# Routed attention and a gated conv FFN on one core: heads prepared in pairs, argmax out of PSUM, shared banks, weights cast on engines, and a new order

## The chip, the cores and the metric

The kernel runs on one core of one Trainium2 chip. The metric is the device time of one launch in microseconds; the kernel before takes 281.45 us (median of three runs, 280.99 to 282.95). Engines are named as in the profile: PE (TensorE, matmuls), PEld (its weight loads), DVE (VectorE), ACT (ScalarE), POOL (GpSimd) and SP (SyncE, which here only issues DMAs). Only PE writes PSUM with matmuls; DVE and ACT read it.

## The reference

Four batches of eight heads, 768 tokens, head size 64; 16 centroids for each head. Queries and keys attend only within their own cluster; the attention output feeds an FFN with a three-tap convolution as its gate. Everything is given in float32.

```python
q_assign = np.argmax(np.einsum('bhsd,hcd->bhsc', q_n, c_n), axis=-1)
k_assign = np.argmax(np.einsum('bhsd,hcd->bhsc', k_n, c_n), axis=-1)
mask = q_assign[:, :, :, None] == k_assign[:, :, None, :]
scores = np.where(mask, scale * np.matmul(q, k.transpose(0, 1, 3, 2)), -1e9)
attn = softmax(scores)                    # over the keys
x = np.matmul(attn, v)                    # -> (4, 768, 512)
h = np.maximum(x @ w_in, 0.0)             # 512 -> 1024
conv_out = sum(conv_w[k] * shifted(h, k - 1) for k in range(3))
return (h * sigmoid(conv_out)) @ w_out    # 1024 -> 512
```

## The kernel before

**Preparing a head.** Each of the 32 heads is loaded by SP into one tile, q and k side by side (`load_q`, `load_k`, L272 and L275: the tile takes pieces of 64 floats, 256 bytes), and v into another (L279). PE transposes six 128x128 blocks against the identity into PSUM (`transposes`, L287). Two copies bring them to SBUF as `qkT` (`qkT_copy`: 512 columns on DVE, L296; 256 on ACT, L294). GpSimd casts to float16 into `ext`, the operand of the scores, directly for the first eight heads (L301) and otherwise into `c16` (L304), from where SP shifts the halves into `ext` by DMA (L306). PE multiplies with the normalised centroids (`assign`, L315, four matmuls that the profile lists as eight).

**The argmax.** DVE transposes the similarities within PSUM (L328), takes the maximum over 16 centroids (L337), compares (L341), multiplies with a descending index (L345), takes the maximum again (L347), and writes codes of the cluster to a small tile `pack` (L349, L351, L355). PE turns `pack` (L360), DVE copies the result (`spk`, L365), and a DMA writes it as three more rows of `ext` (L366). Those rows add to a score a number that is near zero where the clusters agree and very negative elsewhere, so that the exp needs no mask.

**Attention.** The work is cut into 32 slots, one for each batch, query half and head pair. A slot has six steps of scores (two matmuls of 384 columns into one of two double banks `sc`, L424), each followed by an exp on ACT (L436), and six value groups of six matmuls (L442) into the bank `avb`, one slot later. DVE normalises (L454, L455), PE transposes back (L465) and DVE copies into `xT` (L469). The slots go through the four head pairs with one query half and then again with the other, so that heads 0 to 7 serve slots 0 to 7.

**FFN.** When the pairs of a query half are done, eight tiles of the first layer follow (`ffn_in`, L484, into the bank `fp`), each with a relu (L499 on ACT, L497 on DVE), three taps on DVE (L518, L520; at the end on PE, L536), a tanh on ACT (L550), a gate on DVE (L554); the output layer is L560, with a copy out (L572 on ACT, L574 on DVE) and a store by SP (L575). The weights come from DRAM by DMAs that GpSimd issues and that cast on the way (L657, L662).

**PSUM.** Four banks have owners: `tra` and `trb` for preparation, `avb` for values, `fp` for the FFN.

**Order.** Nothing is scheduled automatically: `SLOTS` lists for each slot the steps of all engines in program order, and each engine executes its own in that order. A step waits for the data it needs; what stands behind it on that engine or queue waits too.

Of the kernel before, what the change touches and what calls it, by code (L numbers as in the profile page):

```python
# [801 lines left out]
```

## Time and profile before

| | us |
|---|---|
| median of three runs | 281.45 |
| the profiled execution, span | 281.0 |
| PE busy | 256.6 |
| DVE busy | 233.8 |
| ACT busy | 211.1 |
| POOL busy | 85.7 |
| 16 DMA engines, share of the span, queue of SP | 41.3% |

The slices show a span in 40 parts of 7 us, with the busy share in tenths. The groups list instructions of one line, with the mean duration of one and the idle time ahead of them. The chain follows the last instruction back, at each step to what released it. The timeline lists instructions in order of time, and windows give the busy time of all engines in a stretch. A group's mean includes some 0.1 us in which the next instruction of the engine has already begun, so sums of means lie above the busy time.

### The profile page before, as it was taken

The page shows a single profiled execution, that of the slowest core. Times are in us where ns is not written, and L with a number is a line of the kernel's source. Part 1 is how long each engine was busy: PE and PEld are TensorE (multiplying, and loading weights), DVE is VectorE, ACT ScalarE, POOL GpSimd, SP SyncE. Part 2 cuts the span into 40 slices and gives each one's busy share as a digit, 9 for nine tenths or more (in the row PEclk, how much of TensorE's full clock was granted, in tenths as well). Part 3 has the DMA queues.
Part 4 walks back from the last instruction along what each step waited for, and adds up shares of the span by engine and source line. Part 5 has one row for each costly group of instructions (what it writes and reads, how often), then busy time and mean ns, then how long its engine had stood idle before and what let it go on. Part 6 is the DMA issues. An engine that isn't in the chain of part 4 may idle for free.

```text
span 281.0 us, 7068 instructions
## 1 busy us (share of the span) xinstructions
PE 256.6 (91%) x2605; PEld 160.4 (57%) x2605; DVE 233.8 (83%) x648; ACT 211.1 (75%) x337; POOL 85.7 (30%) x183
## 2 busy tenths in 40 slices
PE   4887695899998999999999989999999999999991
PEld 1444353566755667766666656566566576565540
DVE  4578785478999999999999989989999898897441
ACT  2344584368998979989898879979899999973421
POOL 5783568012326224033563160052142000200000
PEclk9999999579999999999999999999999999999998
DMA  8965549934639468237625765248242110112104
GB/s 162 269 127 90 152 92 166 220 86 110 162 74 158 127 150 219 51 86 182 170 76 137 195 160 126 58 120 220 66 136 56 41 40 0 40 38 77 59 16 149
DMA packets 65816, 32.78 MB, mean 117 GB/s; under 512 B 53491, under 2 KB 62707, under 8 KB 65782
## 3 DMA queue, kind: packets, MB, share of 16 engines
q1 hardware_dynamic: 62184, 29.46, 41.3%
q0 software_dynamic: 2304, 2.10, 5.6%
q10 hardware_dynamic: 1294, 0.77, 0.9%
q8 instruction: 20, 0.33, 0.5%
q14 instruction: 14, 0.11, 0.1%
HBM read 23.11 MB, written 6.29 MB: 105 GB/s over the span
## 4 chain that ended last, share of the span: by engine, by line
PE 69%; DVE 20%; DMA 4%; ACT 3%; issue 2%; DVEq 0%; ACTq 0%
PE sc L424 18%; PE fp L560 10%; PE fp L484 10%; PE avb L442 9%; DVE cnv L520 5%; PE trb L315 4%; PE tra L287 3%; PE sc L560 3%; PE trb L287 3%; DMA ext<-spk 3%; DVE qkT L296 2%; DMA qk_in<-in_k_dram 2%; PE sc L536 2%; PE tra L465 2%; DVE val L345 2%
## 5 line engine op out<-in xcount | busy, mean ns | idle before, releaser
L436 ACT ACTIVATE attn<-sc 128x768 f16<-128x768 f32 x192 | 148.8, 820 | 12.7 <-PE sc L424 11.5
L424 PE MATMUL sc<-ext 128*128 128x384 f16 x384 | 92.3, 335 | 5.0 <-DMA ext<-spk 3.9
L520 DVE SCALAR_TENSOR_TENSOR cnv<-hpad,cwcol,cnv 128x382 f16<-128x382 f16 (+1 forms) x108 | 64.7, 617 | 0.2
L442 PEld LDWEIGHTS <-attn 128*128 128x128 f16 x1152 | 52.7, 99 | 13.8 <-issue 1.9
L442 PE MATMUL avb<-v,attn 128*128 128x65 f16 x1152 | 57.6, 195 | 0.1
L424 PEld LDWEIGHTS <-ext 128*128 128x128 f16 x384 | 33.2, 99 | 26.6 <-issue 11.4
L484 PE MATMUL fp<-xT,w_in 128*128 128x384 f16 x220 | 45.0, 325 | 0.8 <-ACT hpad L499 0.8
L560 PE MATMUL fp<-w_out,hg 128*128 128x512 f16 x144 | 39.2, 379 | 0.0
L554 DVE SCALAR_TENSOR_TENSOR hg<-th,hpad 128x764 f16<-128x764 f32 (+2 forms) x33 | 30.2, 925 | 6.9 <-ACT th L550 6.9
L304 POOL CAST c<-qkT 128x768 f16<-128x768 f32 x24 | 21.7, 906 | 43.0 <-issue 16.9
L309 POOL CAST v<-v_in 128x384 f16<-128x384 f32 x32 | 15.9, 510 | 56.0 <-DMA v_in<-in_v_dram 35.9
L484 PEld LDWEIGHTS <-w_in 128*128 128x128 f16 x256 | 22.8, 97 | 15.6 <-issue 3.3
L499 ACT ACTIVATE hpad<-fp 128x384 f16<-128x384 f32 x51 | 25.7, 504 | 6.1 <-PE fp L484 5.6
L294 ACT ACTIVATE qkT<-trb 128x256 f32<-128x256 f32 x30 | 11.6, 386 | 23.2 <-PE trb L287 8.8
L296 DVE COPY qkT<-tra 128x512 f32<-128x512 f32 x30 | 20.5, 682 | 7.0 <-PE tra L287 6.8
L560 PEld LDWEIGHTS <-hg 128*128 128x128 f16 x192 | 17.1, 97 | 15.5 <-issue 1.2
L550 ACT ACTIVATE th<-cnv 128x764 f32<-128x764 f16 (+1 forms) x27 | 23.1, 855 | 0.1
L287 PE MATMUL tra<-id,qk_in 128*128 128x128 f32 x120 | 20.2, 295 | 1.1 <-DMA qk_in<-in_k_dram 1.1
L455 DVE TENSOR_TENSOR x<-avb,rec 128x384 f16<-128x384 f32 x32 | 17.8, 558 | 1.1
L315 PE MATMUL trb<-qkT,cT 128*32 128x192 f32 x240 | 17.0, 357 | 1.9 <-ACT qkT L294 1.1
L287 PEld LDWEIGHTS tra<-id,qk_in 128*128 128x128 f32 x120 | 15.4, 152 | 5.3 <-issue 2.3
L518 DVE TENSOR_SCALAR cnv<-hpad,cwcol 128x382 f16<-128x382 f16 (+1 forms) x54 | 17.6, 340 | 0.0
(107 smaller groups left out, 287.1 us busy)
## 6 DMA issues: line engine op xcount, KB each, us to landing
qk_in<-in_q_dram SPq DMA_DIRECT2D x32, 192.0 KB
v_in<-in_v_dram SPq DMA_DIRECT2D x32, 192.0 KB
qk_in<-in_k_dram SPq DMA_DIRECT2D x31, 192.0 KB
out_dram<-o_sb SPq DMA_DIRECT2D x22, 256.0 KB
ext<-c SPq DMA_DIRECT2D x48, 96.0 KB
w_in<-in_moe_w_in_dram POOLq DMA_DIRECT2D x8, 128.0 KB, 4.5
w_out<-in_moe_w_out_dram POOLq DMA_DIRECT2D x8, 128.0 KB, 6.9
out_dram<-o_sb ACTq DMA_DIRECT2D x2, 256.0 KB
```

Of the source, the lines that this page charges most:

```text
L287: nc.tensor.transpose(to, qk_t[h][:, j].rearrange("p a d -> p (a d)"), id128[:])
L296: nc.vector.tensor_copy(out=to, in_=bank)
L315: nc.tensor.matmul(sims[32 * j : 32 * (j + 1), :], lhsT=cT32[:, h % H, :], rhs=tokens[:, j], start=True, stop=True, skip_group_check=True,)
L424: nc.tensor.matmul(s[:, i, 0:HS], lhsT=ext_b[h % NE][:, 1, P * (kt + i) : P * (kt + i + 1)], rhs=ext_b[h % NE][:, 0, HS * a : HS * (a + 1) ...
L436: nc.scalar.activation(attn[t, g // 3][:, kt : kt + 2, :], bank_of.pop((t, g))[:, :, 0:HS], AF.Exp, scale=0.125)
L442: nc.tensor.matmul(avp[:, u, 0 : D + 1], lhsT=attn[t, hd][:, kt, P * jq : P * (jq + 1)], rhs=v16_b[(h0 + hd) % NE][:, kt, 0 : D + 1], star ...
L484: nc.tensor.matmul(bank[:, 0:HS], lhsT=w_in16[:, r, 2 * u + f, :], rhs=xT[:, b % 2, r, HS * a : HS * (a + 1)], start=(r == 0), stop=(r == ...
L499: nc.scalar.activation(to, bank[:, 0:HS], AF.Relu)
L520: nc.vector.scalar_tensor_tensor(out=cnv, in0=src, scalar=w, in1=cnv, op0=ALU.mult, op1=ALU.add)
L550: nc.scalar.activation(th_t[n][:, fs, 0:N], pre[:, fs, 0:N], AF.Tanh, scale=0.5)
L554: nc.vector.scalar_tensor_tensor(out=o[:, fs], in0=th_t[n][:, fs, 0:N], scalar=1.0, in1=h[:, fs], op0=ALU.add, op1=ALU.mult)
L560: nc.tensor.matmul(bank[:, 0:Dm], lhsT=hg_b[b][:, fb, P * tq : P * (tq + 1)], rhs=w_out16[:, fb, :], start=(fb == 0), stop=(fb == NFB - 1) ...
```

## The change

The kernel is written anew around head pairs. `PLAN` replaces `SLOTS`: one list of steps, in which `T.3.1@0` is the second group of four transposes of pair 3 into bank 0, `S`/`E`/`V` scores, exps and values, `I`/`O`/`U` the two FFN layers, `Qa`/`Qd`, `Ra`/`Rd`, `Ya`/`Yd`, `Fa`/`Fd` copies, relus and so on with their engine (ACT or DVE), and `_wl`, `_wp`, `_wd`, `_wa` a weight's load and its cast on GpSimd, DVE or ACT.

- **Loads.** One DMA brings q, k or v of two heads (pairs 0 and 1: q and k of one head each). Runs are 768 bytes for q (three tokens) and 1536 for k and v, on both sides. A transposed block now holds two tokens, so the casts and shifts into `ext` write runs of 128 elements (256 bytes) for even and odd blocks; four heads are cast directly (GpSimd, ACT, DVE), 28 by `c16` and DMA. Queries now lie in another order, which the copy into `xT` undoes by writing with a stride of three.
- **Chunks.** A pair's 1536 columns of `qkT` are three copies of 512: 32 on ACT and 16 on DVE in all.
- **Argmax.** The transpose writes to SBUF, all steps but that one read SBUF, the comparison and the product are float16, and each step covers two heads (384 elements; the first four heads one by one). One scaling step is gone (a factor in `scalar2`); a turn and its copy serve two heads.
- **Banks.** `tra`, `trb`, `avb` and `fp` become `flex0` to `flex3`, and `PLAN` names the bank of each use.
- **Weights.** SP loads float32 blocks into buffers that later hold other tiles; 16 casts follow on GpSimd (9), DVE (4) and ACT (3).
- **Engines.** 28 relus are on DVE (9 before) and 36 on ACT; the copies into `xT` are 16 and 16 (all on DVE before); the output copies 12 and 12 (6 and 18 before). The six warm-up matmuls on zeros are gone.

```diff
-SLOTS = {
-    0: (
-        "S0 E0 @zd/10 M1/2 D/3 M2/2 LV/4 S1 M0/3 LK/5 M3/2 LQ/5 M1/3 @wi/1 LQ/6 Ta/4 E1 M4/2 Tb/4 @v/9 QA/4 M5/2 M2/3 "
...
+PLAN = (
+    "E.0.0 K.1.1@2 T.3.1@0 M0.2 CQ.2.1 S.0.1 _wa.2 B.1.1 T.4.0@3 M1.2 BA.1.1 _wp.3 S.0.2 Qd.3.1 E.0.1 CX.2.0 "
...
-    tra = psum.tile([P, 512], F32, name="tra")
-    trb = psum.tile([P, 512], F32, name="trb")
-    avb = psum.tile([P, 512], F32, name="avb")
-    fp = psum.tile([P, 512], F32, name="fp")
+    flex = [psum.tile([P, 512], F32, name=f"flex{i}") for i in range(4)]
+    bank = [x[:] for x in flex] + [sc[i // 2][:, i % 2, :] for i in range(4)]
...
-    def load_q(hh):
-        nc.sync.dma_start(qk_in(hh)[:, :, 0], q[hh // H, hh % H].rearrange("(j p) d -> p j d", p=P))
+    def load_q(g, h=None, queue=nc.sync):
+        b, h0 = batch_pair(g)
+        hs = heads(h)
+        queue.dma_start(
+            qk_in(g)[:, 0, hs].rearrange("p h (a j) d -> p (h a) (j d)", a=2),
+            q[b, h0 + hs.start : h0 + hs.stop].rearrange("h (a p j) d -> p (h a) (j d)", a=2, p=P),
+        )
...
+    def transposes(g, c, at):
+        chunk_at[g, c] = at
+        for i in range(4):
+            h, j = divmod(4 * c + i, J)
+            blocks = qk_t[g][:, j // 3, h, 2 * (j % 3) : 2 * (j % 3) + 2].rearrange("p j d -> p (j d)")
+            nc.tensor.transpose(bank[at][:, P * i : P * (i + 1)], blocks, id128[:])
...
-        for a in range(2):
-            nc.sync.dma_start(ext_b[h % NE][0:D, a, :], c[a * D : (a + 1) * D, :])
+    def ext_blocks(g, h, i):
+        return ext_b[g % NE][0:D, h].rearrange("p a (j t s) -> p t (a j) s", t=2, s=P)[:, i]
...
+    def shift_qk(g, h):
+        c = c_t.pop((g, h))
+        for i in range(2):
+            nc.sync.dma_start(ext_blocks(g, h, i), c[i * D : (i + 1) * D, :].rearrange("p (n s) -> p n s", s=P))
...
-    def sims(h):
-        tb = where[h][1]
-        nc.vector.transpose(tb[:, 0:192], tb[:, 256:448])
...
+        if i == 0:
+            sim_t[key] = rot.tile([P, 384], F32, name="sim", tag="sim", bufs=1)
+            nc.vector.transpose(sim_t[key][:, 0 : G * C], bank[sims_at[key]][:, 0 : G * C])
+        elif i == 1:
+            mx_t[key] = rot.tile([P, 24], F32, name="mx", tag="mx")
+            sim = sim_t[key][:, 0 : G * C].rearrange("p (u c) -> p u c", c=C)
+            nc.vector.tensor_reduce(out=mx_t[key][:, 0:G], in_=sim, axis=AX.X, op=ALU.max)
+        elif i == 2:
+            eq_t[key] = rot.tile([P, 24, C], F16, name="eqq", tag="eqq", bufs=1)
...
+            nc.vector.tensor_tensor(out=eq_t[key][:, 0:G], in0=sim, in1=mx, op=ALU.is_equal)
+        elif i == 3:
+            val_t[key] = rot.tile([P, 24, C], F16, name="val", tag="val", bufs=1)
...
+            nc.vector.tensor_tensor(out=val_t[key][:, 0:G], in0=eq_t.pop(key)[:, 0:G], in1=iota, op=ALU.mult)
...
+    def xT_copy(t, on_act):
+        b, a, pr, g = slot(t)
+        to = xT[:, b % 2, pr, HS * a : HS * (a + 1)].rearrange("p (s j) -> p j s", j=3)
+        src = bank16[x_at[t]][:, 0:HS].rearrange("p (j s) -> p j s", j=3)
...
-            nc.gpsimd.dma_start(
-                w_in16[:, r, f].rearrange("p fb f -> p (fb f)"),
-                moe_w_in[r * P : (r + 1) * P, f.start * P : f.stop * P],
-            )
+    def load_weights(i):
+        if i < 4:
+            nc.sync.dma_start(w_t[i], moe_w_in[P * i : P * (i + 1), :])
+            return
...
+        if name == "wa":
+            nc.scalar.activation(to, src, AF.Copy)
+        else:
+            (nc.gpsimd if name == "wp" else nc.vector).tensor_copy(out=to, in_=src)
```

Three places of the order follow; rows name line, operation, output and inputs, with the size.

SP, the DMA queue, from the shifts of pair 2 to the bias rows of pair 3, in the change (`c` to `ext` is a shift of one head, `spk` to `ext` are bias rows, `w_sb` is a block of weights):

```order
L311 DMA ext_90<-c_345 64x6x128 x2
L311 DMA ext_90<-c_382 64x6x128 x2
L587 DMA w_sb<-in_moe_w_in_dram 128x1024
L271 DMA v_in<-in_v_dram 128x2x384
L255 DMA qk_in<-in_q_dram 128x4x192
L263 DMA qk_in<-in_k_dram 128x2x384
L382 DMA ext_90<-spk 3x12x128 x2
L311 DMA ext_91<-c_488 64x6x128 x2
L311 DMA ext_91<-c_506 64x6x128 x2
L382 DMA ext_91<-spk 3x12x128 x2
```

The same place before, around the bias rows of heads 6 to 8:

```order
L366 DMA ext_91<-spk 3x12x128
L275 DMA qk_in<-in_k_dram 128x6x64
L272 DMA qk_in<-in_q_dram 128x6x64 x2
L275 DMA qk_in<-in_k_dram 128x6x64
L366 DMA ext_92<-spk 3x12x128
L275 DMA qk_in<-in_k_dram 128x6x64
L272 DMA qk_in<-in_q_dram 128x6x64 x2
L279 DMA v_in<-in_v_dram 128x384 x2
L366 DMA ext_93<-spk 3x12x128
```

The bias rows went by head between loads of one head; they now go by pair behind a weight block and the loads of a pair, and the weights stand in SP's queue instead of GpSimd's.

ACT around its first exps, in the change (`qkT` is a chunk copy, `w_in` a weight cast, `attn` an exp):

```order
L293 ACTIVATE v_2_96<-v_in 128x12x64
L382 DMA ext_88<-spk 3x12x128
L287 ACTIVATE qkT<-flex_71 128x512
L608 ACTIVATE w_in_78<-w_sb 128x512
L287 ACTIVATE qkT<-flex_69 128x512
L287 ACTIVATE qkT<-flex_68 128x512
L382 DMA ext_89<-spk 3x12x128
L411 ACTIVATE attn<-sc_66 128x768
L608 ACTIVATE w_in_78<-w_sb 128x512
L382 DMA ext_89<-spk 3x12x128
L411 ACTIVATE attn<-sc_67 128x768
```

Before, the first two exps stood behind two bias-row DMAs and six copies, and no cast; now two casts of loaded v, two casts of weights and four bias-row DMAs stand ahead of or between them.

DVE, from the last argmax of a single head to that of pair 2, in the change:

```order
L365 SCALAR_TENSOR_TENSOR pack_101<-best,pack_101 128x2x6
L289 COPY qkT<-flex_71 128x512
L340 STREAM_TRANSPOSE sim<-flex_69 128x384
L377 COPY spk<-flex_70 36x128
L344 TENSOR_REDUCE mx<-sim 128x24
L289 COPY qkT<-flex_68 128x512
L349 TENSOR_TENSOR eqq<-sim,mx 128x384
L353 TENSOR_TENSOR val<-eqq,iota_77 128x384
L289 COPY qkT<-flex_69 128x512
L340 STREAM_TRANSPOSE sim<-flex_70 128x384
L356 TENSOR_REDUCE best<-val 128x24
```

What took eight steps for each head on 192 elements in PSUM takes eight for two heads on 384 in SBUF, and `spk` is copied once.

More of the change, by code (lines that the diff above doesn't have):

```diff
@@ L274, in load_k @@
-    def load_k(hh, kq=nc.sync):
-        kq.dma_start(qk_in(hh)[:, :, 1], k[hh // H, hh % H].rearrange("(p j) d -> p j d", j=J))
-    def load_v(hh, vq=nc.sync):
-        v_t[hh] = rot.tile([P, J, D], F32, name="v_in", tag="v_in", bufs=6)
-        vq.dma_start(v_t[hh][:], v[hh // H, hh % H].rearrange("(p j) d -> p j d", j=J))
-    qkT, attn, x16, hg_b, hfs, where = {}, {}, {}, {}, {}, {}
-    def transposes(h, js):
-        ta, tb = where[h] = early.get(h) or (tra[:], trb[:])
-        for j in js:
-            to = ta[:, P * j : P * (j + 1)] if j < 4 else tb[:, P * (j - 4) : P * (j - 3)]
-            nc.tensor.transpose(to, qk_t[h][:, j].rearrange("p a d -> p (a d)"), id128[:])
@@ L289, in qkT_copy, with batch_pair, heads @@
-    def qkT_copy(h, part, on_act=False):
-        if h not in qkT:
-            qkT[h] = rot.tile([P, S], F32, name="qkT", tag="qkT", bufs=3)
-        to, bank = ((qkT[h][:, 0:512], where[h][0]), (qkT[h][:, 512:S], where[h][1][:, 0:256]))[part]
+    qk_t, v_t, qkT, chunk_at, c_t = {}, {}, {}, {}, {}
+    sims_at, sim_t, mx_t, eq_t, val_t, turn_at, spk_t = {}, {}, {}, {}, {}, {}, {}
+    def batch_pair(g):
+        return g // NPR, 2 * (g % NPR)
+    def heads(h):
+        return slice(0, 2) if h is None else slice(h, h + 1)
@@ new lines, in turn, with bias_copy, bias_rows @@
+    def turn(g, h, at):
+        turn_at[g, h] = at
+        nc.tensor.transpose(bank16[at][:, 0:P], pack_b[h if h is not None else 2 + g % 3][:], id16[:])
+    def bias_copy(g, h):
+        n = 6 * J * (1 if h is not None else 2)
+        spk_t[g, h] = rot.tile([P, P], F16, name="spk", tag="spk")
+        nc.vector.tensor_copy(out=spk_t[g, h][0:n, :], in_=bank16[turn_at[g, h]][0:n, 0:P])
+    def bias_rows(g, h, queue=nc.sync):
+        spk = spk_t.pop((g, h))
+        for i, hd in enumerate(range(2)[heads(h)]):
+            queue.dma_start(
+                ext_b[g % NE][D : D + BR, hd].rearrange("r a s -> r (a s)"), spk[6 * J * i : 6 * J * (i + 1), :]
+            )
@@ L411, in slot, with scores @@
+    attn, x16, x_at, av_at = {}, {}, {}, {}
     def slot(t):
         b, a, pr = t // SPB, t % SPB // NPR, t % NPR
[L413 to L423 removed]
+        return b, a, pr, b * NPR + pr
+    def scores(t, i):
+        b, a, pr, g = slot(t)
+        h, kt = i // 3, 2 * (i % 3)
+        s = sc[(6 * t + i) % 2]
+        for n in range(2):
@@ new lines, in step @@
+    def step(token):
+        token, _, at = token.partition("@")
+        at = int(at) if at else None
+        name, *args = token.split(".")
+        x = [int(i) for i in args]
+        last = x[1] if len(x) > 1 else None
+        if name[0] == "_":
+            setup(name[1:], at if at is not None else x[0] if x else 0, last)
+        elif name == "L":
+            load_q(x[0])
+            load_k(x[0])
+        elif name == "LQ":
+            load_q(x[0], last)
+        elif name == "LK":
+            load_k(x[0], last)
+        elif name == "La":
+            load_k(x[0], last, nc.scalar)
+        elif name == "LV":
+            load_v(x[0])
+        elif name == "T":
+            transposes(x[0], x[1], at)
+        elif name in ("Qd", "Qa"):
+            chunk_copy(x[0], x[1], name == "Qa")
+        elif name[0:2] == "CD":
+            cast_direct(name, *x)
+        elif name == "CQ":
+            cast_qk(*x)
+        elif name == "CX":
+            shift_qk(*x)
+        elif name[0:2] == "CV":
+            cast_v(name, x[0])
+        elif name == "A":
+            assign(x[0], last, at)
+        elif name[0] == "M":
+            argmax(x[0], last, int(name[1]))
+        elif name == "K":
+            turn(x[0], last, at)
+        elif name == "B":
+            bias_copy(x[0], last)
+        elif name == "BX":
+            bias_rows(x[0], last)
+        elif name == "BA":
+            bias_rows(x[0], last, nc.scalar)
+        elif name == "S":
+            scores(*x)
+        elif name == "E":
+            exps(*x)
+        elif name == "V":
+            values(*x, at)
+        elif name == "N":
+            normalize(x[0])
+        elif name == "X":
+            x_transposes(x[0], at)
+        elif name in ("Yd", "Ya"):
+            xT_copy(x[0], name == "Ya")
+        elif name == "I":
+            ffn_in(*x, at)
+        elif name in ("Rd", "Ra"):
+            relu(*x, name == "Ra")
+        elif name == "C":
+            carry(x[0])
+        elif name in ("a", "b", "c"):
+            tap(*x, "acb".index(name))
+        elif name == "W":
+            conv(*x, at)
+        elif name == "H":
+            tanh(x[0], last)
+        elif name == "G":
+            gate(x[0], last)
+        elif name == "O":
+            ffn_out(x[0], x[1], range(2 * x[2], 2 * x[2] + 2), at)
+        elif name == "U":
+            ffn_out(x[0], x[1], (x[2],), at)
+        elif name in ("Fd", "Fa"):
+            evac(*x, name == "Fa")
+        elif name == "FX":
+            store(*x)
+        elif name == "FY":
+            store(*x, nc.scalar)
```

640 lines of the change are left out of this document (231 added, 409 removed), and 205 rows, old and new, of tables (PLAN, SLOTS).

## The prediction

> **What bounds the kernel now.** I read the page's slices first, then busy time by stage, the waits and the chain in order of time. Slices of 7.0 us:
>
> ```profile
> PE   4887695899998999999999989999999999999991
> ...
> PEclk9999999579999999999999999999999999999998
> ```
>
> From the tenth slice on TensorE (PE) is full; it idles in the first nine and in the last, and its clock drops in slices eight and nine. By stages (columns: time, PE, PE's weight loads, VectorE, ScalarE, GpSimd, each busy us and instructions, then granted clock, DMA share, GB/s):
>
> ```profile
> 0.00:18.30 18.30, 12.37 (x66) 6.49 (x67) 10.81 (x40) 4.57 (x10) 12.21 (x41) 1.00 1.00 212
> 18.30:42.80 24.50, 19.47 (x185) 11.82 (x181) 19.84 (x65) 16.09 (x25) 14.30 (x30) 1.00 0.49 101
> 42.80:50.30 7.50, 3.52 (x58) 2.58 (x58) 3.40 (x10) 2.40 (x5) 5.03 (x9) 0.95 1.05 172
> 50.30:64.30 14.00, 13.98 (x122) 8.91 (x123) 8.98 (x28) 7.75 (x11) 0.96 (x2) 0.66 0.62 138
> 64.30:245.60 181.30, 177.53 (x1959) 114.06 (x1958) 170.92 (x473) 165.52 (x267) 52.53 (x100) 1.00 0.46 115
> 245.60:281.00 35.40, 29.73 (x225) 16.56 (x222) 19.84 (x37) 14.74 (x24) 0.64 (x2) 0.96 0.18 68
> ```
>
> The cuts are exp times. A slot (six exps of a head pair and query half) begins with its first exp: slot 0 in the first row below, slot 5 with the last of the four exps in the second (exps 28 to 31), slot 31 in the third.
>
> ```profile
> 19.33 1.51 ACT L436 ACTIVATE attn<-sc 128x768 f16<-128x768 f32 x2
> ...
> 61.94 3.23 ACT L436 ACTIVATE attn<-sc 128x768 f16<-128x768 f32 x4
> ...
> 245.59 1.51 ACT L436 ACTIVATE attn<-sc 128x768 f16<-128x768 f32 x2
> ```
>
> So slots 0 to 4 take 45.0 us, slots 5 to 30 take 181.3 us (6.97 each) with PE 98%, VectorE (DVE) 94% and ScalarE (ACT) 91% busy, and the rest 35.4 us. The middle is PE's; the start belongs to whoever feeds it:
>
> ```profile
> PE sc L424 <- DMA ext<-spk: 3.9, 1, 3.9
> ```
>
> That wait is one, the longest of PE's. In the chain in order of time and in PE's timeline (start, us, what):
>
> ```profile
> 42.84 7.34 DMA ext<-spk
> ```
>
> ```profile
> 23.37 0.60 PE L287 MATMUL tra<-id,qk_in 128*128 128x128 f32 x4
> ...
> 50.91 1.06 PE L287 MATMUL tra<-id,qk_in 128*128 128x128 f32 x4
> ```
>
> The bias rows of one head are 7.34 us under way while loads fill the DMA engines (share 1.05); PE stands 3.9 us, and then the same four transposes take 1.06 us for 0.60, at a clock of 0.66 over 14 us.
>
> **Stage 1: the start to slot 5 (now 64.3).** Slots 0 to 3 use heads 0 to 7 and slots 4 to 7 use them again, so this stage is paced by how fast heads get ready: transposes on PE, copies out of PSUM on DVE and ACT, the argmax on DVE, a turn on PE, and the DMA of the bias rows. The change does less on DVE for each head. From the same chain, a zeroing of ext and then one head's argmax now:
>
> ```profile
> 25.94 0.70 DVE ext L583
> ...
> 39.52 0.41 DVE trb L328
> 39.95 0.37 DVE mx L337
> ...
> 41.92 0.03 DVE pack L355
> ...
> 42.61 0.21 DVE spk L365
> ```
>
> From L328 to the end of L355 are eight steps in 2.6 us (41.92 plus the 0.17 of such a short step, row L349 below, less 39.52). The new one drops L355: 2.4 us for the four heads done singly. For a pair the long steps double in length. The groups:
>
> ```profile
> L296 DVE COPY qkT<-tra 128x512 f32<-128x512 f32 x30 | 20.5, 682 | 7.0 <-PE tra L287 6.8
> ...
> L328 DVE STREAM_TRANSPOSE trb<-trb 128x192 f32<-128x192 f32 x30 | 11.9, 397 | 5.8 <-PE trb L315 4.4 <-ACT attn L436 0.7
> ...
> L347 DVE TENSOR_REDUCE trb<-val 128x12 f32<-128x192 f32 x32 | 11.4, 357 | 1.3 <-ACT qkT L294 0.8
> ...
> L349 DVE TENSOR_SCALAR pack<-trb 128x12 f16<-128x12 f32 x32 | 5.3, 166 | 1.2 <-ACT qkT L294 0.8
> ...
> L294 ACT ACTIVATE qkT<-sc 128x512 f32<-128x512 f32 x1 | 0.6, 597 | 1.6 <-PE sc L287 1.6
> ```
>
> The added 192 elements cost about 0.20 us (682 for 512 against 397 for 192 is 0.89 ns each). So the transpose is 0.60, four steps 0.55 each, three closing ones 0.17: 3.3 us a pair, 3.5 with one L365, against two times 2.6 plus 0.21, 5.6 in the chain and 5.0 busy. No row has these steps on SBUF sources of 384: if they gain no overlap the pair may cost 4.2, if the f16 product goes at twice the rate 3.2.
>
> First data: the slowest of the first loads lands at 6.5 now; runs are longer, the centroid chain waits too, so 6.0 (5.0 to 6.5). To the first scores DVE then issues a chunk copy 0.7, two zeroings (L583) 1.4, four heads at 2.4, three L365, a second chunk copy, two casts of 64x768 (not in this trace; 0.5 to 0.9 by the same slope) and a copy of 0.2: 14.7 us, plus 1.1 for the first four cold transposes:
>
> ```profile
> 6.64 1.09 PE L287 MATMUL tra<-id,qk_in 128*128 128x128 f32 x4 [1.11 <-DMA qk_in<-in_k_dram]
> ```
>
> First scores at 22, first exp at 23 (19.3 now), **3.7 us later**, but with four heads complete and the transposes of four more issued. Slots 0 to 4 then hold these PE pieces, priced by the chain:
>
> ```profile
> 38.91 0.51 PE trb L315 x8
> ...
> 223.03 0.43 PE fp L560 x2
> ...
> 227.65 0.17 PE tra L465 x3
> 227.82 0.19 PE avb L442 x6
> 228.01 0.33 PE sc L424 x2
> ...
> 230.45 0.65 PE fp L484 x4
> ```
>
> 30 score pairs 9.9, 27 value groups 5.1, 13 groups of four transposes (0.60) 7.8, ten heads of L315 5.1, two L484 groups 1.3, the rest 1: 30.2, plus some 2.5 at the cold clock: 33 us. DVE's share there (seven copies, five and a half pairs, four normalisations, casts) is about 31 by the rows, less where neighbours overlap. Slot 5 starts at **56** instead of 64.3, **8 us earlier**: the 7.5 us stall and the half clock go, the late start takes 3.7 back.
>
> That needs the loads, and it adds waits: on ACT two casts of v and two of weights, and four bias-row DMAs that wait for DVE, stand ahead of chunk copies and of the first two exps, and whoever waits there is the next assignment on PE. At a load rate that keeps up they cost the 0.6 to 0.8 us of each cast, under DVE's 14.7. Before pair 2's bias rows (slot 2, at 36) SP issues 10.3 MB (q and k of seven pairs 5.5, six v pairs 2.4, four blocks of w_in 2.1, two heads shifted 0.4); the rate of full DMA engines now:
>
> ```profile
> 4.00:6.00 2.00, 0.45 (x1) 0.18 (x1) 1.31 (x9) 0.16 (x1) 0.58 (x1) 1.00 1.26 260
> 12.00:14.00 2.00, 1.67 (x11) 1.25 (x7) 1.58 (x8) 0.82 (x2) 1.78 (x7) 1.00 1.10 297
> ```
>
> The first row is q and k alone, in 256-byte pieces; the second is mostly v in 1536-byte runs. From 2 us on, 260 GB/s puts those rows at 42, 297 at 37; q in 768, k and v in 1536, weights in 2048 or more bytes should beat 297. I take no wait; the bound is 6 us.
>
> The Trainium skill, "DMA: Bandwidth & Descriptors", section Specifications, asks for 512 bytes a transfer for line rate; the new shift copies of c into ext break 1536-byte runs into 256, which speaks against the change. At the rate of the 260 row all 5.5 MB of them are 21 us of DMA in some 120, so by the rule as by the row the sum stays.
>
> **Stage 2: slots 5 to 30 (now 181.3).** PE by the same prices: 156 score pairs 51.5, 155 value groups 29.5, 52 L484 groups 33.8, 66 L560 pairs 28.4, 24 transposes groups 14.4, 16 heads of L315 8.2, 26 x 0.17 and nine turns 5: 170.8. About five heads of preparation have moved ahead into stage 1, where PE has room. ACT and DVE by these groups:
>
> ```profile
> L436 ACT ACTIVATE attn<-sc 128x768 f16<-128x768 f32 x192 | 148.8, 820 | 12.7 <-PE sc L424 11.5
> ...
> L499 ACT ACTIVATE hpad<-fp 128x384 f16<-128x384 f32 x51 | 25.7, 504 | 6.1 <-PE fp L484 5.6
> ...
> L469 DVE COPY xT<-tra 128x384 f16<-128x384 f16 x32 | 11.2, 349 | 1.1 <-PE tra L465 1.0
> ...
> L497 DVE TENSOR_SCALAR hpad<-fp 128x384 f16<-128x384 f32 x4 | 2.2, 556 | 1.2 <-PE fp L484 1.2
> ```
>
> Over the whole kernel the 192 exps stay (148.8 us). ACT loses 19 relus (-9.6) and six output copies of 512 (-3.6), gains 16 xT copies priced as L499 (+8), 32 chunk copies of 512 for 32 mostly of 256 (+6) and nine casts and zeroings (+6): about +7 of the 211 us that the stages sum to. DVE loses 1.5 us of busy time a pair in the argmax (-21), 14 chunk copies (-9.5), 16 xT copies (-5.6) and three zeroings (-2), gains 19 relus (+10.6), six output copies (+4) and six casts (+4); its 16 remaining xT copies now write f16 with a stride of three, which no row shows: 0.35 if the stride is free, 0.56 as the relu of L497 if it costs the fast copy, and I take the upper (+3). Together -17 of the 234 that the stages sum to. GpSimd issues 16 weight DMAs less and makes nine more casts; it is busy 52.5 of 181.3 us here, so that hides. Both fuller engines stay under PE, if narrowly. With PE at the 98% of now, 174; I take **175** (170 if nothing waits, 181 as now): 6 us gained.
>
> **Stage 3: from slot 31 (now 35.4).** The last units, their convolutions on PE, output matmuls and stores are the same in number, and the last store leaves behind the last copy as now. PE is busy 29.7 of 35.4 us. I leave 35.4; 34 if the new order fills a wait behind the last gates, 37 if it opens one.
>
> Sum: 56 + 175 + 35.4 = 266.4 on a span of 281.0; the median of the runs lies 0.4 above it. **267 us.**
>
> **Rivals.** *The loads are late.* For it: 10.3 MB must come by 36, while now the first 18.3 us move 212 GB/s; and ACT's casts hold the exps when a weight is late. At 260 GB/s the wait is 6 us and the clock falls as after 50.3, some 5 us more: 278. The Trainium skill, "TensorE: Matmul & The Clock Gate", Part 1, has half clock after an idle window of 3.4 us and full clock after a busy one. The 3.9 us wait agrees, the return does not: 0.66 over 14 us means about 9.5 us at half. By the rule this rival would be 275 or so. *The argmax gets no cheaper* or DVE was never what PE waited for: stage 2 stays at 181.3: 273. *Banks turn too tightly*, the slower one: values, FFN, transposes and assignments share four banks, so each of some 160 bank uses in stage 2 waits for an eviction queued on an engine that is over 90% busy. Today values own avb and the FFN owns fp. If one turn in three costs PE half a microsecond, an L499 or L497, that is 27 us: 294. It decides from 18 us of such waits. Against it: PE's rows in the new order rarely refill a bank next to its reader.
>
> **Numbers.** Forecast 0.58, late loads 0.17, no relief 0.15, banks 0.10. The range 260 to 281 holds 170 for stage 2 with an early start, and the two rivals that gain. Faster by over 1% (about what a measurement tells from no change; under 278.6): the forecast, no relief, and half of the late loads, 0.81; within 1% 0.10; slower 0.09.
>
> **What would show it.** First exp near 23, slot 5 near 56, no ext<-spk wait of PE over 1 us, PEclk full from about 26 on; DVE near 218, ACT near 218; slots of 6.7 us. PE waiting on ACT or DVE evictions in the middle for more than 10 us, or a clock of 0.5 in a slice after slot 0, would make it wrong.

## The result, and the profile after

The changed kernel takes 274.1 us in the median of its runs (272.0 to 277.7), the kernel before 282.2 beside it. The ratio, which leaves out the one run that counts as slow (277.7), is 0.969, 95% interval 0.961 to 0.976. Forecast were 267 us, range 260 to 281. The profiled execution is the fastest of the four, 272.0 us with a span of 270.2; the forecast for the span was 266.4.

The slices (6.75 us each) of the changed kernel:

```profile
PE   1768878699979979999999999998999999999994
...
PEclk9979999689999999999999999999999999999999
DMA  7999969889975951242633130222111100112014
```

There still is a dent in PE and its clock in the eighth slice, and PE is full only from the sixteenth on. The exps give the cuts, as in the prediction: the first; slot 5 (exp 31); slot 12 (exp 73), a cut added here; and slot 31 (exp 187, at 237.47, the second of the last row's three).

```profile
22.45 0.81 ACT L411 ACTIVATE attn<-sc 128x768 f16<-128x768 f32 x1
...
61.57 0.81 ACT L411 ACTIVATE attn<-sc 128x768 f16<-128x768 f32 x1 [0.20 <-PE sc L399]
...
112.71 0.79 ACT L411 ACTIVATE attn<-sc 128x768 f16<-128x768 f32 x1
...
236.66 2.33 ACT L411 ACTIVATE attn<-sc 128x768 f16<-128x768 f32 x3 [0.33 <-PE sc L399]
```

The stages of the changed kernel (time, then PE, PE's weight loads, DVE, ACT and POOL, each busy us and instructions, then clock, DMA share, GB/s):

```profile
0.00:22.45 22.45, 12.55 (x106) 8.84 (x106) 16.21 (x51) 11.77 (x19) 11.17 (x42) 0.92 0.95 321
22.45:61.57 39.12, 32.41 (x385) 22.28 (x378) 30.41 (x75) 29.26 (x41) 16.45 (x21) 0.91 0.93 230
61.57:112.71 51.14, 46.77 (x543) 31.88 (x540) 49.47 (x107) 46.96 (x73) 33.95 (x45) 1.00 0.68 176
112.71:237.47 124.76, 122.98 (x1360) 79.54 (x1359) 121.33 (x265) 118.24 (x175) 20.25 (x34) 1.00 0.23 65
237.47:270.20 32.73, 28.91 (x213) 15.65 (x209) 11.13 (x18) 18.12 (x29) 0.76 (x5) 1.00 0.20 73
```

The same stages of the kernel before, up to slot 31 (the last stage stands in the prediction):

```profile
0.00:19.33 19.33, 13.39 (x69) 7.01 (x70) 11.80 (x43) 5.59 (x10) 13.14 (x44) 1.00 0.96 203
19.33:64.35 45.02, 35.99 (x359) 22.84 (x358) 31.28 (x98) 25.27 (x39) 19.37 (x38) 0.89 0.63 126
64.35:113.13 48.78, 46.92 (x538) 30.27 (x536) 46.86 (x136) 44.02 (x74) 17.48 (x33) 1.00 0.64 147
113.13:245.59 132.46, 130.55 (x1424) 83.74 (x1422) 124.00 (x338) 121.44 (x194) 35.05 (x67) 1.00 0.39 103
```

Slot 12 starts at almost the same time in both profiles, 113.1 and 112.7. Nearly all of the gain lies behind it: 7.7 us in slots 12 to 30, 2.7 in the last stage. In slots 12 to 30 PE is busy 98.6% of the time in both kernels; it has 7.6 us less to do. The transposes of q and k (PE alone, same stage) show what is missing, in the kernel before and in the changed one:

```profile
113.13:245.59 132.46, 13.56 (x83) 1.00 0.39 103
```

```profile
112.71:237.47 124.76, 6.25 (x44) 1.00 0.23 65
```

39 transposes fewer, at six a head; the same view has 80 assignment matmuls for 112, at eight a head, and six turns for fifteen. (Busy time by line counts pipelined ends twice, so these add up to more than 7.6.) So the changed kernel has transposed six and a half more heads and assigned four more when slot 12 begins, and turns them in pairs. PE is not busier for it in that time, in which it idles in both kernels: 91.7 us of 112.7 (12.55, 32.41 and 46.77) for 96.3 of 113.1 (13.39, 35.99 and 46.92). The six warm-up matmuls that are gone were 2.1 us of that; the rest was not followed up. No run moves the preparation back: for this cause the evidence is the count, and the run below that gives PE more to do.

### The profile page after: what moved, and what is told of

Read it like the earlier page. It is cut to its first block, busy times and chain, and to the rows that moved or that the text cites. A ratio compares the mean times of both kernels' runs of the same rounds, so it can differ in the third digit from the quotient of the medians.

```text
span 270.2 us, 6772 instructions
## 1 busy us (share of the span) xinstructions
PE 243.6 (90%) x2585; PEld 158.2 (59%) x2585; DVE 228.6 (85%) x511; ACT 224.3 (83%) x336; POOL 82.6 (31%) x146
## 4 chain that ended last, share of the span: by engine, by line
PE 47%; DVE 28%; DMA 10%; issue 4%; POOL 4%; ACT 2%; SPq 2%; DVEq 0%; POOLq 0%; ACTq 0%
PE sc L399 11%; PE flex L555 11%; PE flex L475 9%; PE flex L423 7%; DVE cnv L511 7%; DMA w_sb<-in_moe_w_out_dram 3%; DMA ext<-c 3%; PE flex L280 3%; DVE hg L543 3%; DMA qk_in<-in_k_dram 3%; POOL taps L698 2%; DVE x L437 2%; DVE cnv L509 2%; PE sc L517 2%; DVE xT L457 2%
## 5 line engine op out<-in xcount | busy, mean ns | idle before, releaser
L411 ACT ACTIVATE attn<-sc 128x768 f16<-128x768 f32 x192 | 151.2, 820 | 10.7 <-PE sc L399 8.1
L399 PE MATMUL sc<-ext 128*128 128x384 f16 x384 | 94.7, 328 | 3.1 <-ACT attn L411 1.7
L511 DVE SCALAR_TENSOR_TENSOR cnv<-hpad,cwcol,cnv 128x382 f16<-128x382 f16 (+1 forms) x108 | 67.0, 644 | 0.4
L423 PE MATMUL flex<-v,attn 128*128 128x65 f16 x1152 | 64.5, 194 | 0.0
L475 PE MATMUL flex<-xT,w_in 128*128 128x384 f16 x256 | 51.3, 325 | 0.4 <-DVE hpad L490 0.4
L555 PE MATMUL flex<-w_out,hg 128*128 128x512 f16 x176 | 51.4, 378 | 0.0
L306 POOL CAST c<-qkT 128x768 f16<-128x768 f32 x28 | 27.5, 985 | 63.9 <-DMA ext<-c 34.3
L543 DVE SCALAR_TENSOR_TENSOR hg<-th,hpad 128x764 f16<-128x764 f32 (+2 forms) x33 | 32.3, 980 | 11.2 <-ACT th L535 11.1
L280 PE MATMUL flex<-id,qk_in 128*128 128x128 f32 x192 | 32.1, 302 | 2.3 <-DVE xT L457 1.3
L280 PEld LDWEIGHTS flex<-id,qk_in 128*128 128x128 f32 x192 | 24.2, 155 | 6.2 <-DVE xT L457 1.7
L287 ACT ACTIVATE qkT<-flex 128x512 f32<-128x512 f32 x32 | 19.2, 608 | 5.7 <-PE flex L280 3.9
L488 ACT ACTIVATE hpad<-flex 128x384 f16<-128x384 f32 x36 | 18.3, 508 | 3.9 <-PE flex L475 3.1
L698 POOL TENSOR_SCALAR taps<-id,cwcol 128x128 f16<-128x128 f16 x24 | 19.5, 821 | 0.0
L437 DVE TENSOR_TENSOR x<-flex,rec 128x384 f16<-128x384 f32 x32 | 17.8, 557 | 1.1
L490 DVE TENSOR_SCALAR hpad<-flex 128x384 f16<-128x384 f32 x28 | 15.3, 550 | 3.5 <-PE flex L475 3.2
```

What stands on the lines that cost most here:

```text
L280: nc.tensor.transpose(bank[at][:, P * i : P * (i + 1)], blocks, id128[:])
L306: nc.gpsimd.tensor_copy(out=c_t[g, h][:], in_=qkT[g][:, h, :])
L399: nc.tensor.matmul(s[:, n, 0:HS], lhsT=ext_b[g % NE][:, h, 1, P * (kt + n) : P * (kt + n + 1)], rhs=ext_b[g % NE][:, h, 0, HS * a : HS * ( ...
L411: nc.scalar.activation(attn[t, i // 3][:, kt : kt + 2, :], sc[(6 * t + i) % 2][:, :, 0:HS], AF.Exp, scale=0.125)
L423: nc.tensor.matmul(avp(at)[:, u, 0 : D + 1], lhsT=attn[t, h][:, kt, P * jq : P * (jq + 1)], rhs=v16_b[g % NE][:, h, kt, 0 : D + 1], start= ...
L437: nc.vector.tensor_tensor(out=x16[t].rearrange("p jq (h d) -> p h jq d", h=2), in0=av[:, :, 0:D].rearrange("p (h jq) d -> p h jq d", h=2), ...
```

## The experiments

Times are ratios to the kernel before; the change itself has 0.969. Stages come from one profile each. One run below (the last stores) equals the change up to its last matmuls: there slots 0 to 4 took 38.8 us, slots 5 to 11 52.2, and slot 12 began at 114.6, so differences under 2 us ahead of slot 12 mean nothing. Behind it the profiles agree far better: slots 12 to 30 take 124.8 us, within 0.05, in the change and in the four runs below that leave them as they are (later weights, casts later, pair 8 first, the last stores).

### What held slots 0 to 4

Forecast were 33 us for them with no wait; they took 39.1 with PE idle for 6.7. PE's waits there (us in total, times, longest):

```profile
PE sc L399 <- ACT attn L411: 1.4, 2, 1.2
PE flex L448 <- DVE x L437: 1.2, 1, 1.2
PE sc L399 <- DMA ext<-spk: 1.2, 1, 1.2
PE flex L372 <- DVE pack L365: 1.1, 3, 0.5
PE flex L280 <- DMA qk_in<-in_k_dram: 0.8, 1, 0.8
PE flex L323 <- DVE qkT L289: 0.6, 1, 0.6
PE flex L280 <- DMA qk_in<-in_q_dram: 0.3, 1, 0.3
```

and pieces of the chain in order of time (start, us, what):

```profile
30.38 7.14 DMA qk_in<-in_k_dram
...
37.54 0.75 SPq L382
...
38.82 6.02 DMA w_sb<-in_moe_w_out_dram
...
44.86 0.43 DVE w_out L610
```

The timelines of SP and of PE have pair 2's bias rows and the scores that need them:

```profile
30.97 1.67 SPq L382 DMA_DIRECT2D ext<-spk  x2
```

```profile
37.96 0.48 PE L399 MATMUL sc<-ext 128*128 128x384 f16 x2 [1.16 <-DMA ext<-spk]
```

k of pair 6 is 7.14 us under way, and only then SP issues the second of pair 3's bias rows. Pair 2's bias rows, some 9 KB each, were issued at 30.97 right behind that k, and PE could go on with them only at 37.96. DVE waits for a weight block before it casts it, and the normalisation that follows is what PE waits for at 49.1; ACT stands at another such cast. Only 2.3 us of PE's 6.7 are waits on a DMA itself; the rest are on ACT and DVE. Was it the weights?

**Output weights later.**

```diff
-S.2.1 _wl.5 V.1.3@1 ... _wl.4 ... _wp.10 _wl.6 ... _wd.11 L.7 E.2.5
+S.2.1 L.7 V.1.3@1 ... E.2.5
 (six loads _wl.4 to _wl.9 now in slots 3 to 5, their eight casts in slots 6 to 8)
```

> The change with its order altered in slots 2 to 8 only: the q and k loads of pair 7 are issued ahead of any block of the output weights, the six blocks of the output weights follow in slots 3 to 5, and their eight casts stand in slots 6 to 8 instead of 2 to 5. In the changed kernel slots 0 to 4 took 39.1 us (22.45 to 61.57) where 33 was forecast; PE stood 6.7 us of them, of which 1.0 on q and k of pair 7, 1.2 behind a DVE that had waited 1.3 us for a weight block, 1.2 behind exps on an ACT that had waited 0.8 us for another, and then ran at a granted clock of 0.66 to 0.81. Theory (the weight blocks and their casts hold up these slots): slot 5 starts at 57 to 58.5, granted clock near 1.00 from 48 to 60, no wait of PE on qk_in, and the span falls by 3 to 4.5 us, to about 266. Rival (the chain through the argmax and the turn paces these slots, weights or not): slot 5 still at 60.5 to 62 and the span within 1 us of 270.

Measured: ratio 0.983 (0.977 to 0.988), slower than the change. Stages, and PE's longest wait:

```profile
24.20:58.46 34.26, 30.17 (x389) 21.32 (x380) 27.74 (x70) 28.19 (x40) 11.87 (x15) 0.96 0.72 178
58.46:118.57 60.11, 49.78 (x543) 33.91 (x540) 49.50 (x110) 47.78 (x75) 30.47 (x48) 0.91 0.73 186
```

```profile
PE flex L280 <- DMA qk_in<-in_q_dram: 6.4, 1, 6.4
```

The theory holds for slots 0 to 4, 34.3 us, near the 33 of the forecast. But slots 5 to 11 lose more than that, 60.1 for 51.1: the blocks now stand ahead of q of a later pair.

**Casts later, blocks in place, q and k of pair 7 ahead of the first block; then pair 8 loaded before pair 10 as well.**

```diff
-S.2.1 _wl.5 V.1.3@1 ... _wd.11 L.7 E.2.5     (casts in slots 2 to 5)
+S.2.1 L.7 _wl.5 V.1.3@1 ... E.2.5            (casts in slots 6 to 8)
```

```diff
-B.6 L.10 Qd.7.1 ... c.0.1 L.8 b.0.0
+B.6 L.8 Qd.7.1 ... c.0.1 L.10 b.0.0
```

> The change with two things moved: the eight casts of the output weights stand in slots 6 to 8 instead of 2 to 5 (as in the run with later weights), and q and k of pair 7 are issued ahead of the first block of the output weights; the weight blocks themselves keep their places in SP's queue, unlike there, where slots 0 to 4 took 34.3 us but PE then stood 6.4 us at 69 for q of a pair queued behind the delayed blocks. Theory (DVE and ACT stood at casts of blocks that had not landed, and pair 7 was late; the loads as a whole fit): slots 0 to 4 take 34 to 36 us instead of 39, slots 5 to 11 stay at 51 to 52, the whole falls by 3 to 5 us against the changed kernel, to 268 to 270 in the median. Rival (all loads up to slot 7 share full DMA engines, so whatever goes ahead makes another late): slots 0 to 4 gain, slots 5 to 11 lose about as much, the whole stays within 1.5 us of the changed kernel's 273.

> As the run with the casts moved, and besides q and k of pair 8, whose transposes come first (slot 6), are loaded where those of pair 10 stood (slot 4), and those of pair 10 (transposes in slot 7) where those of pair 8 stood. Theory (order of need): slots 5 to 11 lose the 1.3 to 1.7 us waits on a late pair, 49 to 51 us, and the whole is 0.5 to 2 us under the run with the casts moved. Rival (the transposes of slots 6 and 7 do not wait on loads but on banks and DVE): no difference above 0.5 us.

Measured: 0.986 (0.980 to 0.992) and 0.982 (0.975 to 0.988). Slots 0 to 4 took 36.5 and 37.3 us; slots 5 to 11, of the first and of the second:

```profile
60.53:118.61 58.08, 48.92 (x542) 33.20 (x539) 52.25 (x110) 47.45 (x74) 34.55 (x48) 0.94 0.68 173
```

```profile
60.79:115.91 55.12, 47.20 (x542) 31.77 (x539) 52.66 (x110) 47.57 (x74) 37.30 (x48) 1.00 0.65 176
```

The rival is right, and worse: slots 0 to 4 gain 2 to 3 us, slots 5 to 11 lose 4 to 7. Loading pair 8 first removes a 4.7 us wait of PE on q, as its theory said, and slot 12 still starts at 115.9. DVE has 3 us more work in slots 5 to 11 now, where it had been busy 49.5 of 51.1 us; that this is what holds them is likely, not shown.

**Weights by GpSimd's casting DMAs, as before the change.**

```diff
-nc.sync.dma_start(w_t[i], moe_w_in[P * i : P * (i + 1), :])
+nc.gpsimd.dma_start(w_in16[:, i, f]..., moe_w_in[P * i : P * (i + 1), f.start * P : f.stop * P])
-... 16 casts _wp, _wd, _wa
```

> The change with the weights loaded as in the kernel before: 16 DMAs of 128 KB that GpSimd issues and that cast on the way, at the places where the blocks were loaded, and none of the 16 casts on GpSimd, DVE and ACT and none of the ten blocks in SP's queue. Theory (the blocks in SP's queue and the casts that wait for them are what made slots 0 to 4 take 39 us instead of 33): slots 0 to 4 take 34 to 36 us, slot 12 starts at 108 to 110 instead of 112.7 to 114.6 (the changed kernel and the run that differs from it in the last stores only), and the whole falls by 3 to 5 us. Rival (the same bytes cross the same full DMA engines, whichever queue carries them): slots 0 to 4 within 1.5 us of 39, slot 12 at 112 to 115, and the whole within 1.5 us; if GpSimd's issuing delays its casts of q and k, slot 12 comes later than 115.

Measured: 0.966 (0.958 to 0.974), no different from the change. Slots 0 to 4 and 5 to 11:

```profile
26.44:64.47 38.03, 32.79 (x393) 22.99 (x386) 26.41 (x70) 27.80 (x40) 13.60 (x20) 0.88 0.81 174
64.47:115.80 51.33, 47.32 (x542) 31.82 (x539) 49.68 (x107) 46.88 (x73) 31.61 (x44) 1.00 0.64 172
```

Mostly the rival's figures: 38.0 us, without one weight cast on any engine; PE now waited 2.7 us for q of pair 7 there. Slot 12 came at 115.8, later than its 112 to 115, because the first exp came late, at 26.4, behind a 4.2 us wait of PE on the convolution's weights. So the way of the weights bought nothing and cost nothing in all. What paces the first twelve slots is no single wait: each one taken away brought another. Which resource would have to grow stays open.

### Long runs

**q, k and v in 256-byte pieces.** In that order of tokens the copies into xT are plain.

```diff
-q[...].rearrange("h (a p j) d -> p (h a) (j d)", a=2, p=P)
+q[...].rearrange("h (j p) d -> p (h j) d", p=P)      (k and v alike)
```

> The change with q, k and v read in pieces of 256 bytes (one token each) instead of 768 and 1536, and with the copy into xT writing its columns one behind the other, which this loaded order asks for; so it differs from the run with plain xT copies only in the runs of the loads. Theory (the loads are short of time in the first 50 us and long runs were needed): the first scores and slot 5 come later than in the run with plain copies, slot 5 by 3 us or more, PE waits on qk_in or on bias rows for more than 4 us and its clock drops again; the time is 4 us or more above that run, and at least that of the changed kernel. Rival (the DMA engines have room, queue order and buffers set when a load starts): the time is within 1.5 us of the run with plain copies.

Measured: 1.035 (1.029 to 1.042), against 0.960 for plain copies with long runs (below): 20 us. The first exp comes at 31.1, slot 12 at 134.8; slots 12 to 30 take 123.4. The same 16 us of both, first this run and then the change:

```profile
4.00:20.00 16.00, 7.84 (x54) 5.27 (x54) 9.20 (x24) 5.61 (x11) 6.04 (x23) 0.94 1.35 218
```

```profile
4.00:20.00 16.00, 10.26 (x77) 7.12 (x77) 12.19 (x35) 8.68 (x14) 6.27 (x23) 0.89 1.05 354
```

The DMA engines are full in both and move 218 GB/s in 256-byte pieces, 354 in long ones. Without the long runs the changed kernel is slower than the one before. The Trainium skill, "DMA: Bandwidth & Descriptors", Specifications, asks for at least 512 bytes for line rate: the two rates agree.

### Who sets the middle

**More work for PE; more work for DVE.**

```diff
-for jq in range(3):
+for jq in (0, 1, 2, 0, 1, 2):          (first run)
```

```diff
+for _ in range(2):                     (second run)
     nc.vector.reciprocal(out=rec[:], in_=av[:, :, D : D + 1])
```

> The change with each of the 96 X matmuls issued twice (the second writes the same), so PE alone gets more to do: 0.17 us more for each three by the chain's row, 32 times in all, 19 of them in slots 12 to 30, 3.2 us there. In the changed kernel slots 12 to 30 (112.71 to 237.47) take 124.8 us with PE busy 123.0, DVE 121.3 and ACT 118.2. Theory (PE sets these slots; the change gained here because PE has less left to do): slots 12 to 30 go to 128 us, the whole by about 5 us, to some 278. Rival (DVE, nearly as busy, sets them): 125 to 126, the whole by 1 to 2.

> The change with the reciprocal of each normalisation issued twice, so DVE alone gets more to do: 0.185 us 32 times, 19 of them in slots 12 to 30, 3.5 us there. Theory (PE sets slots 12 to 30 and DVE has room behind it): these slots stay within 1 us of 124.8, slots 5 to 11, where DVE was busy 49.5 of 51.1 and PE 46.8, go up by at most 1.3, and the whole by 1 to 2. Rival (DVE sets the middle): slots 12 to 30 go to 128 and the whole by 4 to 6.

Measured: 0.985 (0.980 to 0.989) and 0.988 (0.982 to 0.994). Slots 12 to 30 of the first and of the second:

```profile
114.43:241.91 127.48, 125.60 (x1414) 82.40 (x1413) 121.79 (x265) 118.97 (x176) 19.87 (x34) 1.00 0.22 63
```

```profile
116.73:245.12 128.39, 124.53 (x1360) 79.12 (x1359) 124.24 (x284) 118.79 (x176) 21.07 (x34) 1.00 0.22 63
```

For some 3.2 us of PE the stage grew by 2.7; for 3.5 us of DVE by 3.6, the rival's figure. I had given DVE room behind PE, and that fell: the 3.4 us that it idles in 124.8 did not take in 3.5 us of work. This work stands between the values and the X matmuls, so the run cannot tell DVE's load from a longer delay on that path. Either addition lengthens the stage.

**The argmax one head at a time.**

```diff
-nc.vector.transpose(sim_t[key][:, 0 : G * C], bank[sims_at[key]][:, 0 : G * C])
+for x in range(n): nc.vector.transpose(sim_t[key][:, cols], bank[sims_at[key]][:, cols])    (each step alike)
```

> The change with each step of the argmax of a pair issued twice on 192 columns, one head at a time, from the same SBUF tiles; turn, bank use and the order stay. By the chain's rows of the first heads such a step takes 0.36 to 0.39 us (transposition, maximum, comparison, second maximum), 0.27 (product) and 0.18, so a pair costs about 1.1 us more on DVE: 14 pairs 15 us, of which 5 in slots 0 to 4, 3 in slots 5 to 11 and 6 in slots 12 to 30. Theory (DVE holds the kernel along with PE, as the run with a second reciprocal says, so pairs were needed for the gain): the whole goes up by 9 to 14 us, to 282 or more, no faster than the kernel before, with slots 12 to 30 at 129 to 131. Rival (the second reciprocal hurt as a delay between the values and the X matmuls, not as DVE time; DVE's other work gives way): slots 12 to 30 at most 127 and the whole up by 6 or less.

Measured: 0.975 (0.969 to 0.981), slots 12 to 30:

```profile
116.40:241.17 124.77, 123.30 (x1360) 79.46 (x1359) 121.75 (x300) 118.33 (x175) 21.19 (x34) 1.00 0.23 65
```

DVE's busy time rose by 0.4 us here, not by 6: two steps of 192 columns back to back overlap, and cost little more than one of 384. The theory was not put to the test, its price was wrong; and in slots 12 to 30 the width of the steps is not what the pairs brought. What was lost lies ahead of slot 5 (42.2 us for 39.1); the two ratios' intervals overlap.

**Plain copies into xT; reordering by PE's writes; reordering by PE's reads.**

```diff
-to = xT[...].rearrange("p (s j) -> p j s", j=3)
+to = xT[...]
```

```diff
-nc.tensor.transpose(bank16[at][:, P * jq : P * (jq + 1)], x16[t][:, jq, :], id16[:])
+nc.tensor.matmul(bank[at][:, jq:HS:3], lhsT=x16[t][:, jq, :], rhs=id16[:], ...)
```

```diff
-rhs=ext_b[g % NE][:, h, 0, HS * a : HS * (a + 1)]
+rhs=ext_b[g % NE][:, h, 0, HS * a : HS * (a + 1)].rearrange("p (j s) -> p s j", j=3)
```

> The change without the reordering in the copy into xT: 384 columns are written one behind the other instead of with a stride of three, so the rows of each query half stay in the loaded order; nothing else differs. In the changed kernel such a copy takes 0.80 us on DVE and 0.82 on ACT, 16 each, against 0.35 on DVE before. Expected of the copies by both theories: 0.35 on DVE and about 0.50 on ACT, so DVE -7 and ACT -5 us. Theory (in the middle DVE, 97% busy, holds PE through the wait of the X transposes on the normalisation, 4.0 us there): slots 5 to 30 fall from 175.9 to 170 to 172, the span by 4 to 6. Rival (PE's own work of 170 us sets the middle and both engines only fill their slack): the span falls by 1.5 us or less.

> The change with the reordering moved from the copy into xT to PE: the three X matmuls write float32 into the bank with a stride of three, and the copy reads 384 float32 and writes float16 one behind the other. Expected of the copy: 0.55 on DVE and 0.50 on ACT, as the relus L490 and L488 of the same size (0.55, 0.51), so DVE -4 and ACT -5 us. If PE writes with a stride at no cost, X x3 stays 0.17 to 0.22 us. Theory (DVE holds the middle): the span falls by 2.5 to 4. Rival (PE sets it): by 1 or less; and if the strided write costs PE time, X x3 is 0.3 us or more and the span rises by 3 or more.

> The change with the reordering of the queries moved from the copies into xT to the scores: their moving operand is read from ext in steps of 128 elements by threes, so all that follows is in token order and the copies into xT are plain (0.35 us on DVE and 0.49 on ACT, as in the run with plain copies). If PE reads such an operand at full rate (0.33 us a pair) the time is that of the run with plain copies, 2 to 3 us under the changed kernel; if it reads at half the rate, 192 pairs cost 0.33 us more each, some 60 us in all, and slots 12 to 30 take 160 us or more.

Measured: 0.960 (0.953 to 0.967), 0.979 (0.972 to 0.986), 1.197 (1.193 to 1.200). The copies of the change, and of the run with plain ones (mean ns behind the busy time):

```profile
L455 ACT ACTIVATE xT<-flex 128x384 f16<-128x384 f16 x16 | 13.1, 821 | 2.7 <-PE flex L448 2.5
L457 DVE COPY xT<-flex 128x384 f16<-128x384 f16 x16 | 12.8, 802 | 0.6 <-PE flex L448 0.5
```

```profile
L455 ACT ACTIVATE xT<-flex 128x384 f16<-128x384 f16 x16 | 7.9, 491 | 3.2 <-PE flex L448 2.9
...
L457 DVE COPY xT<-flex 128x384 f16<-128x384 f16 x16 | 5.6, 352 | 1.1 <-PE flex L448 1.0
```

The plain run leaves out the reordering, so its queries stay in the loaded order: it is a probe of the time only. Without the stride DVE and ACT lose 7 and 5 us, some 4 and 3 of them in slots 12 to 30, and these shrink by only 1.3 (to 123.5). Slots 5 to 30 fall to 174.3, not to the 170 to 172 of the theory (the medians differ by more, some 2.5 us of the whole by the ratios, but those intervals overlap). In the change PE idles only 1.8 of the 124.8 us, so relief for the engines behind it has little to give. With the reordering on PE, which also writes float32 there, the X matmuls take 302 ns in the mean for 221, and slots 12 to 30 grow to 126.4. Reading ext by threes costs far more (the scores' group there):

```profile
L399 PE MATMUL sc<-ext 128*128 128x384 f16 x384 | 177.0, 542 | 0.6 <-ACT attn L411 0.6
```

against 94.7 us, 328 ns. The stride in the copies is the cheapest place of the three.

### The end

**Output tiles that end together.**

```diff
-U.3.5.4@1 U.3.3.5@5 G.31.1 U.3.4.4@2 U.3.3.6@5 ... U.3.3.7@5 U.3.4.6@2 Fa.3.3 ... Fa.3.4 ... Fa.3.5 ... Fa.3.2 FX.3.2
+U.3.4.4@2 U.3.5.4@1 U.3.2.4@4 G.31.1 U.3.3.5@5 ... U.3.2.7@4 Fa.3.3 Fd.3.4 FY.3.3 FX.3.4 Fa.3.5 Fd.3.2 FY.3.5 FX.3.2
```

> The change with its last output steps in the order of the kernel before: the four open output tiles take their last matmuls by turns and end together, and their copies follow on ACT and DVE by turns and their stores from two queues, instead of one tile after the other. In the changed kernel the last matmul ends near 266.3 and the span 3.9 us later; before it was 275.3 and 5.7. Theory (1.8 of the 2.7 us that the last stage gained is this finish): slot 31 to the end goes from 32.7 to 34 to 35, the rest unchanged. Rival (the gain is PE work that was moved ahead, and the finish hides): within 0.5 us of 32.7.

Measured: 0.980 (0.975 to 0.985); the last stage goes from 32.7 to 34.0 us (to the span's end at 273.3). In the other runs that keep the change's finish and its matmuls it takes 32.6 to 33.1. So the finish (its order, the engines of the copies and the queues of the stores, changed together) is 0.9 to 1.4 of the 2.7 us gained there.

No run here beats the change: the one with casting DMAs equals it, and the one with plain copies leaves out the reordering.

## Why the prediction was right, and where not

The time lies in the range and the way was right, but the gain did not come from where the forecast had it. By the profiles, stage 1 was to give 8.3 us and gave 2.8, stage 2 was to give 6.3 and gave 5.3, and stage 3 gave 2.7 where nothing was forecast: that quarter of the gain is luck. The median alone would not tell the forecast (267) from "no relief" (273); stage 2 does, at 175.9 for 181.3.

- **Stage 1, forecast 56, measured 61.6.** The first exp was forecast at 23 and came at 22.45; an argmax of a pair at 3.5 us on DVE, and the means of its rows for pairs add up to 3.6 (0.57, 0.54, 0.62, 0.45, 0.54, 0.22, twice 0.21, 0.21). (192 elements at 0.89 ns are 0.17 us, not the 0.20 taken; it made no difference.) PE's work in slots 0 to 4 with the cold clock was put at 32.7 and was 32.4. The step that failed is "I take no wait; the bound is 6 us": PE idled 6.7. The rate of the loads was not at fault: 321 GB/s to 22.45 and the 259 of this stretch are 10.7 MB by 36 us, 10.3 were wanted.

```profile
22.45:36.00 13.55, 11.70 (x152) 8.27 (x148) 12.95 (x35) 10.85 (x17) 7.66 (x10) 1.00 1.02 259
```

  What I left out is that SP's queue and the casts tie loads to what stands behind them: bias rows that are under way for 7 us behind a load, as one was in the kernel before, and a normalisation behind a cast. Later weights gave 34.3.
- **Stage 2, forecast 175, measured 175.9.** PE's sum was 170.8 and 169.75 is its busy time. That preparation moved ahead of it, to where PE has room, was the right reason. But the one pace of 6.7 us a slot hid two: slots 5 to 11 take 7.3 each, longer than before (51.1 for 48.8; DVE is busy 49.5 of them), and slots 12 to 30 made up for it with 6.6.
- **DVE 218 and ACT 218, measured 228.6 and 224.3.** The argmax saved the 21 us; its groups are 59.0 after and 80.2 before. The strided copies cost 0.80 and 0.82 instead of 0.56 and 0.50: 3.9 and 5.1 us. The three taps and the gates also got slower on DVE (L511 644 ns for 617, L543 980 for 925), 4.4 us; why is not settled, and some 2 us of DVE and 1 of ACT stay open.
- **Stage 3, forecast 35.4, measured 32.7.** I counted the matmuls, not how the last tiles end: about half of it by the run above. PE is busy 0.8 us less there (28.9 for 29.7).
- **The median** lies 3.9 us above the profiled span, not 0.4 as before: the profiled execution was the fastest. With the 3.8 us on the span this makes the 7 us between 267 and 274.1.
- **Rivals.** Late loads came half true: the idle time is near what it was priced at (6.7 for 6), by chance, since most of it is not on a load itself; and the 5 us for the clock did not come on top, since PE's busy time is the forecast's with its 2.5 us of cold clock. Banks that turn too tightly did not come: all waits of PE in slots 5 to 30 are these, and on a bank's eviction only the second and the third, 1.7 us where 18 were needed.

```profile
PE flex L448 <- DVE x L437: 4.0, 6, 1.7
PE flex L280 <- DVE xT L457: 1.3, 1, 1.3
PE flex L475 <- DVE hpad L490: 0.4, 1, 0.4
PE sc L399 <- ACT attn L411: 0.2, 1, 0.2
```

  "No relief" is nearer than I gave it: taking some 7 us from DVE and ACT in slots 12 to 30 bought 1.3 there.
- **Signs.** The first exp and the pace of 6.8 us a slot came as forecast, and none of the signs against came as it was put. Slot 5, DVE and ACT missed, PE waited 1.2 us for bias rows, and its clock was at half from 49.84 to 56.67, which in slices of 6.75 us reads as 0.6 and 0.8.

## What to carry to other kernels

Cut the span where the idle engine becomes the full one, and count its instructions on both sides: a reorder gains what it moves from the full part into the part with room, and little for work saved on the engines behind it (here 1.3 us for 7). A wait in an overfull prologue is worth what the next one leaves of it; run the fix before you count its gain. And before a load is made cheaper by another layout, price the stride that undoes it on each engine that could.

## What the runs showed of the hardware

PE's granted clock changes in steps of 3.41 us, and PE need not stand still for it to halve. Four steps of the changed kernel:

```profile
46.42:49.84 3.42, 1.22 (x13) 0.68 (x13) 3.19 (x6) 2.59 (x5) 2.97 (x5) 1.00 1.07 348
49.84:53.25 3.41, 2.37 (x14) 1.42 (x13) 1.29 (x5) 1.35 (x3) 0.98 (x2) 0.50 0.94 119
53.25:56.67 3.42, 3.42 (x21) 2.62 (x19) 1.01 (x3) 2.02 (x3) 1.59 (x2) 0.50 0.45 113
56.67:60.10 3.43, 3.36 (x58) 2.28 (x57) 3.26 (x8) 2.46 (x4) 0.00 (x0) 1.00 0.96 313
```

A step with 1.22 us of work, cut by two waits of 1.2 us, is followed by half clock; a step at half clock with 2.37 does not end it, here a full one does. In the run with single heads 1.60 of 3.40 was also too little. A full step does not always end it: in the kernel before, a step that was full at half clock was followed by another at half.

```profile
53.00:56.40 3.40, 3.40 (x24) 2.34 (x23) 2.25 (x9) 1.62 (x2) 0.00 (x0) 0.50 0.86 228
56.40:59.85 3.45, 3.45 (x38) 2.54 (x36) 1.99 (x6) 1.62 (x3) 0.96 (x2) 0.50 0.21 53
```

The Trainium skill, "TensorE: Matmul & The Clock Gate", Part 1, has a window of 3413 ns, which agrees. It has the return after a busy window, which agrees in the changed kernel and not in the one before; and it has the drop after an idle window, where the first rows show it after one that was a third busy.
